# Attention feeding a squared-ReLU layer: batch 0's queries turned on TensorE and its second scores taken token-major

## The chip, the cores and the metric

The kernel runs on one core of a Trainium2 chip. A core has TensorE (PE in the profile; PEld is its weight load), VectorE (DVE), ScalarE (ACT), GpSimd (POOL) and SyncE (SP), each with its own in-order queue of instructions, a memory SBUF of 128 partitions, an accumulator memory PSUM that TensorE writes, and 16 DMA engines. The metric is the device time of one execution in microseconds (us), the median over several.

## The reference

```
def sm_attn(qq, kk, vv):                     # per batch (8) and head (8)
    s = scale * matmul(qq, kk.T)             # scale = 1/8
    a = softmax(s)                           # over the last axis
    return matmul(a, vv)
p_packed = sm_attn(p, k, v)                  # 32 packed queries against 576 tokens
attn     = sm_attn(q, p_packed, p_packed)    # 576 tokens against the 32 packed rows
x = attn.transpose(0, 2, 1, 3).reshape(4608, 512)
out = square(relu(x @ w_in)) @ w_out         # 512 -> 2048 -> 512
```

Each tensor q, k, v is 8 x 8 x 576 x 64 in float32, p is 8 x 8 x 32 x 64.

## The kernel before

**Tiling.** The eight heads of a batch are two quads of four. The 32 packed rows of four heads fill 128 partitions, so one quad is one tile. Tokens of a batch are 576 = 18 x 32 (S, T, NP). For batches 0 and 1 the tokens are cut into half A of 256 and half B of 320 (CUTS, line 40), for the others into two of 288.

**Stages of one batch.** k is turned on DVE in 32x32 blocks of 32-bit pairs (`kT`), first scores s1 on TensorE, their maximum `m1` on DVE, exponential `x1` on ACT with its sum, transpose `eT` on TensorE, copy `eo` out of PSUM, product with v `pv`, division `pp` (reciprocal `rd` before it). The packed rows pp are turned twice: `pt`/`po` give ppT through TensorE and a copy, `bd` gives ppd in 32x32 blocks on DVE. Then the second attention: q turned on DVE (`qA`, `qB` for the halves, line 363), second scores (`zA`, `zB`, line 375) with the packed rows on the partitions and the tokens along the free axis, a DVE transpose of the scores to have tokens on the partitions (`tA`, line 518), maximum `mA`, subtraction `sA`, exponential `xA`, sum and reciprocal `uA`, weighting `aA`, and a transpose back (`TA`, line 563) to a2T. These seven steps run once for each quad and half. The product of packed rows with w_in is formed once per batch (`wa`, `wb`, `w0`, `w1`, with copies `Wa` and so on), so that the first layer is `h` = wp x a2T: for each block of 128 features two matmuls, one a quad. `r` is the ReLU out of PSUM, `q` with dots the square into gT, `o` the second layer, two matmuls a word, `c` its copy and `d` the store.

**What sets the order.** ORDER (lines 50 to 132) is a list of words written out by hand, 1,451 of them; `run` executes them in this order, and each engine works its own instructions off in it. A letter behind the colon gives the engine (a ACT, p POOL, v or none DVE). A word such as `qA01` names the step, batch and quad; `h0.1.8` batch, half and feature block. `Z18.0` issues 18 matmuls on zeros of 512 columns and none of 256, which write to a PSUM bank that nobody reads (`busy`, line 333). Loads stand in the list too: `Lk`, `Lv`, `LA`/`LB` (q's halves), `Wi` (w_in in six pieces: column part 0, 1 or 2, then the row half), `Wo` (w_out in quarters) on POOL's queue, `pf` (p of the first two batches) on SP's. POOL's transfers use eight semaphores in turn, so a transfer is issued when the one eight places ahead of it has landed. The second layer of the first four token tiles takes w_out's quarters in the order 0, 2, 1, 3.

**PSUM.** Four banks of the pool `psa` make two double buffers (tag a) that s1, second scores and wp share; the other four hold small tiles and the zeros' target in the first stage (`spare`, `idle`), and later x and y for h and o. Batch 0's even blocks use x, its odd ones y.

Of the kernel before, what the change touches and what calls it, by code (L numbers as in the profile page):

```python
# [9 lines left out]
ALU = mybir.AluOpType  # L10
# [11 lines left out]
D = 64  # L22
# [12 lines left out]

WIDE = range(2, 8)
# [20 lines left out]
q0.1.0:v r0.1.8:a h0.1.10 W100:v W101:a h0.1.11 h0.1.3 q0.1.4:p h0.1.2 r0.1.10:a r0.1.3:v r0.1.11:a h0.0.4 kT10 r0.1.2:a  # L57
LB1 h0.0.13 r0.0.4:a h0.0.5 q0.1.1:a h0.1.14 r0.0.13:v q0.1.5:p h0.0.14 r0.0.5:v h0.1.13 r0.1.14:a kT11 h0.0.15
r0.0.14:a h0.0.6 q0.0.2:a h0.0.12 Wo1 r0.0.15:v s11 r0.1.13:a r0.0.12:v r0.0.6:a Wo3 h0.1.15 q0.0.7:v q0.0.6:a h0.0.7
r0.1.15:v h0.1.4 r0.0.7:a Lv20 h0.1.6 m110 r0.1.4:a h0.1.5 r0.1.6:a h0.1.7 m111 h0.1.12 q0.0.3:a o2.0 x110 r0.1.5:v o2.1  # L60
r0.1.12:v q0.1.7:p o0.0 x111 o3.0 r0.1.7:a eT10 q0.1.6:a o0.1 Pr q0.1.2:v eT11 q0.1.3:v eo10:a o1.0 rd1 eo11:v o3.1 pv1
o1.1 pp1 o0.2 pt1 o1.2 bd1 po1:a o3.2 qA11 w011 w111 qA10 W011:a o0.3 W111:v o2.2 Lv21 o1.3 qB10 zA1 qB11 w010 o2.3 tA11
W010:a tA10 o3.3 mA11 zB1 mA10 sA11 w110 o0.4 sA10 tB11 W110:a o2.4 tB10 o1.4 mB11 xA11 o0.5 xA10 mB10 o1.5 uA10 o2.5
Lk20 sB11 o0.6 uA11 o0.7 xB11 aA10 o1.6 c0:a aA11 o1.7 sB10 o3.4 TA10 c1:a d0 TA11 o2.6 uB11 xB10 h1.0.1 Lk21 h1.0.6 Px
o2.7 r1.0.1:v d1 r1.0.6:v o3.5 aB11 h1.0.0 c2:a h1.0.2 Pt o3.6 r1.0.0:a TB11 o3.7 r1.0.2:a d2 Lk31 Pu:v q1.0.0:a h1.0.4
h1.0.3 c3:a o4.0 r1.0.3:v r1.0.4:a o5.0 kT20 q1.0.1:a h1.0.7 d3 h1.0.5 uB10 o5.1 r1.0.5:a o4.1 r1.0.7:v q1.0.2:a aB10
h1.0.10 h1.0.8 q1.0.3:v r1.0.10:a o4.2 kT21 Lq2 h1.0.9 r1.0.8:a o5.2 r1.0.9:a h1.0.12 TB10 s12 q1.0.4:v r1.0.12:a
h1.0.14 m120 o5.3 Lv30 r1.0.14:a h1.1.1 m121 h1.1.3 r1.1.1:a o5.4 x120 r1.1.3:v h1.0.11 o4.3 r1.0.11:v x121 h1.1.7 kT31
h1.0.15 eT20 Lq3 q1.0.5:a o4.4 r1.0.15:v eT21 r1.1.7:v q1.0.7:a o5.5 rd2 eo20:v eo21:a h1.0.13 h1.1.2 r1.0.13:v o4.5
r1.1.2:v q1.0.6:a h1.1.6 pv2 r1.1.6:v h1.1.8 pp2 h1.1.0 q1.1.1:a r1.1.8:v Lk30 o5.6 qT21 q1.1.3:a o4.6 h1.1.12 r1.1.0:a  # L70
bd2 pt2 qT20 o4.7 bs2:a Lk40 h1.1.5 po2:v r1.1.12:a o5.7 q1.1.0:v c4:a h1.1.10 r1.1.5:v c5:a s22 d4 r1.1.10:v h1.1.4
o6.0 t221 r1.1.4:a h1.1.9 d5 o7.0 q1.1.2:a t220 h1.1.13 r1.1.9:a o6.1 qT30 r1.1.13:a Lq4 h1.1.11 q1.1.4:a m221 w120 w121
r1.1.11:a o6.2 m220 W121:a h1.1.14 h1.1.15 W120:v Lv31 o6.3 r1.1.14:a q1.1.6:a o7.1 o6.4 sb21:v r1.1.15:a Lv40 o7.2
q1.1.5:a kT30 o7.3 q1.1.7:a o7.4 sb20:v Lk41 x221 o6.5 qT31 o7.5 x220 o6.6 su21 o6.7 o7.6 su20 c6:a o7.7 w020 a221 c7:a
d6 w021 o8.0 W020:a a220 o8.1 d7 o8.2 aT21 W021:a o8.3 aT20 o8.4 Lq5 h2.0.1 h2.0.0 r2.0.1:v o8.5 r2.0.0:a o8.6 q2.0.0
h2.0.2 h2.0.3 r2.0.2:v o9.0 Lk50 o8.7 r2.0.3:v h2.0.5 c8:a s13 q2.0.1 r2.0.5:a h2.0.4 d8 m130 o10.0 r2.0.4:a h2.0.6 kT40
h2.0.7 r2.0.6:a o10.1 r2.0.7:a q2.0.2 h2.0.10 Lk51 x130 m131 o9.1 h2.0.8 r2.0.10:a q2.0.3 o9.2 r2.0.8:a kT41 h2.0.13
x131 eT30 h2.0.9 r2.0.13:v o10.2 eo30:a rd3 r2.0.9:v h2.1.1 eT31 q2.0.4 h2.0.14 r2.1.1:a o10.3 r2.0.14:v eo31:a h2.0.11
Lk61 o9.3 r2.0.11:v o9.4 h2.0.12 h2.1.5 q2.0.5 r2.0.12:a pv3 r2.1.5:v h2.0.15 q2.0.6 h2.1.4 pp3 r2.0.15:a o9.5 r2.1.4:v
h2.1.6 bd3 pt3 q2.0.7 h2.1.0 bs3:a o9.6 r2.1.6:v r2.1.0:v Lv41 po3:a o9.7 q2.1.2 h2.1.8 q2.1.0 c9:a h2.1.2 r2.1.8:v s23  # L80
# [54 lines left out]
class Kernel:  # L135
# [128 lines left out]
    def load_rows(self, x, s, n=0, engine=None):  # L264
# [558 lines left out]
```

## Time and profile before

| | |
|---|---|
| median of 3 runs | 243.33 us (243.23 to 243.66) |
| the profiled execution | 243.35 us, span from first to last instruction 241.5 us |
| busy time PE / DVE / ACT / POOL | 235.4 / 203.0 / 142.0 / 74.8 us |
| first 512-column matmul on zeros | 1.19 us |
| first product of the first layer (batch 0, half A) | 21.28 us |
| first product of half B | 24.45 us |
| first second-layer matmul (o2.0) | 33.0 us |
| first product of batch 1 (h1.0.1) | 48.8 us |
| matmuls on zeros (L335) | 59, 16.1 us |
| landing of k00, k01, v00, v01, q half A | 6.05, 7.7, 9.2, 10.65, 12.1 us |
| landing of w_in's four narrow pieces, q half B | 13.3, 14.6, 18.0, 19.3; 17.0 us |
| landing of w_out's quarters 0, 2, 1, 3 | 30.2, 35.6, 41.0, 43.5 us |

Starts are from the timeline, in us from the first instruction. A landing is the issue's start plus the time to landing in the view of transfers. Busy TensorE time includes the matmuls on zeros, so it does not tell how much of it is needed work. A wait on an engine that is not the bottleneck costs nothing.

### The profile page before, as it was taken

How to read it: one execution, taken by the hardware profiler on the slowest of the kernel's cores; microseconds unless marked ns; L12 is line 12 of the kernel's file. 1: busy time of each engine (PE TensorE's matmuls, PEld its weight loads, DVE VectorE, ACT ScalarE, POOL GpSimd, SP SyncE). 2: the span in 40 equal slices, each digit the busy share in tenths (PEclk: the TensorE clock that was granted, in tenths of full speed). 3: DMA queues.
4: the chain of work that ended last, by engine and by line, in shares of the span. 5: the costliest groups of instructions: out<-in, count | busy, mean ns of one | idle time of the engine just before them, and what ended most of it. 6: DMA issues, size and time to landing. Idle time of an engine off the chain costs nothing.

```text
span 241.5 us, 6098 instructions
## 1 busy us (share of the span) xinstructions
PE 235.4 (97%) x2415; PEld 125.9 (52%) x2415; DVE 203.0 (84%) x459; ACT 142.0 (59%) x308; POOL 74.8 (31%) x123
## 2 busy tenths in 40 slices
PE   8998899999999999999999999999999999999994
PEld 3544564456544564456555554465545644555542
DVE  2679986999998889989998889997899879987740
ACT  2216993697897557955693647774495346733300
POOL 8637783594585262044303340002000000000000
PEclk9999999999999999999999999999999999999999
DMA  6999999999999979259932974217113111111224
GB/s 103 189 199 210 202 206 206 181 209 210 194 169 212 236 103 136 51 71 209 107 86 28 206 107 66 62 34 105 37 24 76 46 46 43 43 46 43 50 61 109
DMA packets 33404, 28.51 MB, mean 118 GB/s; under 512 B 8160, under 2 KB 28384, under 8 KB 33376
## 3 DMA queue, kind: packets, MB, share of 16 engines
q0 software_dynamic: 26848, 18.55, 54.2%
q1 hardware_dynamic: 6384, 9.51, 14.8%
q8 instruction: 19, 0.31, 0.5%
q14 instruction: 9, 0.07, 0.1%
q10 hardware_dynamic: 144, 0.07, 0.1%
HBM read 37.22 MB, written 9.44 MB: 193 GB/s over the span
## 4 chain that ended last, share of the span: by engine, by line
PE 91%; DMA 4%; ACT 2%; DVE 1%; SPq 0%; issue 0%; POOL 0%; POOLq 0%
PE ps_o L648 50%; PE ps_h L590 26%; PE ps_wp L574 4%; PE ps_idle L335 3%; PE ps_s L375 3%; DMA k_b<-in_k_dram 2%; PE ps_e1T L433 2%; PE ps_pv L457 1%; DMA out_dram<-o_sb 1%; ACT r L595 1%; ACT wp L419 1%; SPq L679 0%; PE ps_ppT L496 0%; ACT gT L633 0%; DVE kT L351 0%
## 5 line engine op out<-in xcount | busy, mean ns | idle before, releaser
L648 PE MATMUL ps_o<-w_out_bf,gT 128*128 128x512 bf16 (+1 forms) x576 | 147.3, 378 | 0.0
L590 PE MATMUL ps_h<-a2T,wp 128*128 128x288 bf16 (+2 forms) x512 | 89.9, 286 | 1.3 <-DVE rs L543 0.6
L595 ACT ACTIVATE r<-ps_h 128x288 bf16<-128x288 f32 (+2 forms) x159 | 61.0, 415 | 47.2 <-PE ps_h L590 42.5
L648 PEld LDWEIGHTS <-gT 128*128 128x128 bf16 x576 | 54.4, 98 | 43.1 <-issue 3.4
L590 PEld LDWEIGHTS <-wp 128*128 128x128 bf16 x512 | 47.7, 98 | 42.4 <-issue 8.0
L597 DVE TENSOR_SCALAR r<-ps_h 128x288 bf16<-128x288 f32 (+2 forms) x97 | 41.9, 447 | 11.1 <-PE ps_h L590 10.5
L635 DVE TENSOR_TENSOR gT<-r 128x576 bf16<-128x576 bf16 (+2 forms) x104 | 45.1, 446 | 2.8 <-ACT r L595 1.8
L419 ACT CAST wp<-ps_wp 128x1024 bf16<-128x1024 f32 (+1 forms) x29 | 27.7, 974 | 9.0 <-PE ps_wp L574 8.9
L419 ACT COPY o_sb<-ps_o 128x512 f32<-128x512 f32 x26 | 15.2, 589 | 12.3 <-PE ps_o L648 10.1
L268 POOL DMA_DIRECT2D k_b<-in_k_dram x28 | 15.2, 544 | 16.5 <-DVE kT L351 7.3
L268 POOL DMA_DIRECT2D q_b<-in_q_dram x16 | 11.0, 690 | 28.8 <-DVE qT L363 25.4
L313 POOL DMA_DIRECT2D v_b<-in_v_dram x12 | 9.4, 779 | 31.5 <-PE ps_pv L457 30.5
L335 PE MATMUL ps_idle<-gT 128*128 128x512 bf16 (+1 forms) x59 | 16.1, 417 | 1.2 <-DVE gT L187 1.2
L413 ACT ACTIVATE e<-ps_s,nm 128x576 bf16<-128x576 f32 x16 | 11.8, 742 | 7.5 <-DVE nm L401 7.4
L633 ACT ACTIVATE gT<-r 128x512 bf16<-128x512 bf16 (+1 forms) x21 | 14.0, 690 | 0.5 <-DVE r L597 0.3
L535 ACT ACTIVATE e<-d 128x576 f32<-128x576 f32 (+2 forms) x20 | 11.7, 599 | 4.1 <-DVE d L529 3.9
L351 DVE STREAM_TRANSPOSE kT<-k_b 128x576 uint32<-128x576 uint32 x16 | 12.3, 767 | 0.6 <-DMA k_b<-in_k_dram 0.6
L363 DVE STREAM_TRANSPOSE qT<-q_b 128x576 uint32<-128x576 uint32 (+2 forms) x20 | 12.4, 633 | 0.0
L541 DVE TENSOR_REDUCE sums<-e 128x18 f32<-128x576 f32 (+2 forms) x20 | 12.2, 608 | 0.1
L401 DVE TENSOR_REDUCE nm<-ps_s 128x1 f32<-128x576 f32 x16 | 11.5, 739 | 0.8 <-PE ps_s L375 0.7
L523 DVE TENSOR_REDUCE mx<-s 128x18 f32<-128x576 f32 (+2 forms) x20 | 11.6, 609 | 0.0
L529 DVE TENSOR_TENSOR d<-s,mx 128x576 f32<-128x576 f32 (+2 forms) x19 | 11.6, 631 | 0.0
(60 smaller groups left out, 179.3 us busy)
## 6 DMA issues: line engine op xcount, KB each, us to landing
out_dram<-o_sb SPq DMA_DIRECT2D x65, 128.0 KB, 2.9
v_b<-in_v_dram POOLq DMA_DIRECT2D x12, 256.0 KB, 5.5
w_out_bf<-in_moe_w_out_dram POOLq DMA_DIRECT2D x4, 512.0 KB, 12.4
q_b<-in_q_dram POOLq DMA_DIRECT2D x6, 288.0 KB, 5.3
q_b<-in_q_dram POOLq DMA_DIRECT2D x12, 144.0 KB, 5.7
k_b<-in_k_dram POOLq DMA_DIRECT2D x12, 108.0 KB, 4.1
gT<-in_v_dram POOLq DMA_DIRECT2D x4, 288.0 KB, 9.7
w_in_bf<-in_moe_w_in_dram POOLq DMA_DIRECT2D x4, 256.0 KB, 9.8
```

The costliest lines, as they stand in the source:

```text
L268: engine.dma_start(x[n:], s[:P - n])
L335: self.nc.tensor.matmul(ps[:, :m], lhsT=self.nought[:, :P], rhs=self.nought[:, :m], start=True, stop=True)
L351: self.nc.vector.transpose(t["kT"][:].rearrange("p s e -> p (s e)").bitcast(U32), t["k"][:].rearrange("p t d -> p (t d)").bitcast(U32))
L363: self.nc.vector.transpose(out.bitcast(U32), x.bitcast(U32))
L419: engine.copy(out, x)
L541: nc.vector.reduce_sum(out=sums[:, x], in_=t["e2"][:, x], axis=AX.X)
L590: self.nc.tensor.matmul(ps, lhsT=t["wp"][:, fb // n, fb % n * P:(fb % n + 1) * P], rhs=t["a2T"][:, s0:s1], start=(qd == 0), stop=(qd == se ...
L595: engine.activation(r, ps, ACT.Relu)
L597: engine.tensor_scalar_max(r, ps, 0.0)
L633: engine.activation(out, r, ACT.Square)
L635: engine.tensor_tensor(out=out, in0=r, in1=r, op=ALU.mult)
L648: self.nc.tensor.matmul(self.o[tt][:, e], lhsT=self.gT[:, fb, a:a + P], rhs=self.w_out_bf[:, fb, e], start=(i == 0), stop=(i == self.NFB - 1))
```

## The change

Five things are changed.

1. **Queries of batch 0** are no longer turned on DVE. TensorE turns them with the identity into PSUM (`QA`, `QB`: 4 or 5 transposes for a quad and half) and a copy brings them to SBUF (`EA`, `EB`: three of the four on ACT, one on DVE). Two tokens of 64 features now fill the 128 partitions.
2. **Second scores of batch 0** (`yA`, `yB`) have 32 tokens of one head as weights and ppT as the moving operand, so that each matmul gives a block of 32 tokens x 32 packed rows with the tokens on the partitions. Half A takes 64 such matmuls and half B 80, in place of 16 each. The DVE transposes of the scores (`tA`, `tB`) and ppd of batch 0 (`bd`) are not made.
3. **The softmax** of batch 0's second attention runs for both quads in one instruction: `MA` maximum and `SA` subtraction straight from PSUM, `XA` exponential in place, `UA` sum and reciprocal, and the same for B. The exponentials are kept in float32 in an unused part of gT. Only the weighting `AA` is still one instruction a quad, all four now on DVE (three of the four were on POOL, with one subtraction).
4. **The early part of ORDER** is new, up to the first words of batch 1's first layer: 269 words become 259, and the last 1,182 words are the same steps on the same engines. p's first loads are split: batch 0's on ACT's queue ahead of its table load, batch 1's on SP's. On POOL's queue the order is k00, k01, q half A, v00, v01, q half B, the six pieces of w_in, then batch 1's k, w_out's first quarter, and batch 1's v and q. There are 24 matmuls on zeros in place of 59.
5. **Other engines** for some batch 0 steps: an e1T copy and a wp copy go to ACT and ppT's copy to DVE, and several ReLUs and squares change places between ACT, DVE and POOL.

The functions that are new:

```diff
+    def st_qP(self, t, qd, hf):
+        n = self.span(hf)
+        x = self.q_part(t["q"], n)[:, qd]
+        m = (n.stop - n.start) // 2
+        ps = t["ps_q", hf] = self.bank16(0, "ps_q")[:, :m * P].rearrange("p (u c) -> p u c", c=P)
+        for u in range(m):
+            self.nc.tensor.transpose(ps[:, u, :], x[:, 2 * u:2 * u + 2, :].rearrange("p t d -> p (t d)"), self.ident)
+
+    def st_qE(self, t, engine, hf):
+        n = self.span(hf)
+        y = self.new(t, self.tp, "qT", [P, T // 2, P], BF16)
+        self.copy(engine, y[:, n.start // 2:n.stop // 2, :], t["ps_q", hf])
+
+    def st_z(self, hf):
+        n = self.span(hf)
+        m = (n.stop - n.start) // 2
+        ps = self.turn32("ps_z")[:, :, :self.NQ * m * NP].rearrange("p e (q u i) -> p e q u i", q=self.NQ, i=NP)
+        self.att[0, 0]["ps_z", hf] = ps
+        for u in range(m):
+            for qd in range(self.NQ):
+                t = self.att[0, qd]
+                for h in range(QH):
+                    g = NP * self.group(qd, h)
+                    for e in range(2):
+                        r = slice(D * e, D * e + D)
+                        self.nc.tensor.matmul(ps[g:g + NP, e, qd, u, :],
+                                              lhsT=t["qT"][r, n.start // 2 + u, NP * h:NP * h + NP],
+                                              rhs=t["ppT"][r, NP * h:NP * h + NP], start=True, stop=True)
+
+    def st_zmax(self, hf):
+        ps = self.att[0, 0]["ps_z", hf]
+        self.nc.vector.tensor_reduce(out=self.z_small("mxz", hf), in_=ps, op=ALU.max, axis=AX.X)
+
+    def st_zsub(self, hf):
+        ps, d = self.att[0, 0]["ps_z", hf], self.z_work(hf)
+        self.nc.vector.tensor_tensor(out=d, in0=ps, in1=self.z_small("mxz", hf).unsqueeze(4).to_broadcast(list(d.shape)), op=ALU.subtract)
+
+    def st_zexp(self, hf):
+        d = self.z_work(hf)
+        self.nc.scalar.activation(d, d, ACT.Exp, scale=SCALE)
+
+    def st_zsum(self, hf):
+        x, y = self.z_small("smz", hf), self.z_small("rsz", hf)
+        self.nc.vector.reduce_sum(out=x, in_=self.z_work(hf), axis=AX.X)
+        self.nc.vector.reciprocal(y, x)
+
+    def st_za2(self, engine, hf, qd):
+        t, n = self.att[0, qd], self.span(hf)
+        e2, rs = self.z_work(hf)[:, :, qd], self.z_small("rsz", hf)[:, :, qd]
+        a2 = self.new(t, self.tp, "a2", [P, T // 2, NP, 2], BF16)
+        engine.tensor_tensor(out=a2[:, n.start // 2:n.stop // 2].rearrange("p u i e -> p e u i"), in0=e2,
+                             in1=rs.unsqueeze(3).to_broadcast(list(e2.shape)), op=ALU.mult)
```

`z_work` is the float32 view of gT, `z_small` a small tile for each half. The order, up to half B's first product and the words just behind it:

```diff
-pf Lk00 Lk01 Lv00 Lv01 I P0 LA0 P1 Wi00 kT00 Wi10 LB0 Z18.0 s100 Wi01 kT01 Wi11 m100 Z2.0 s101 x100 m101 Wi21 x101 Z7.0
-eT00 eo00:v Z1.0 eT01 rd0 eo01:v Wi20 Z2.0 pv0 pp0 qA01 Lk10 Z2.0 pt0 bd0 qA00 po0:a Z2.1 zA0 Lk11 tA00 tA01 mA01 mA00
-sA01:v xA01 sA00:v uA01 xA00 qB00 Wo0 qB01 aA01:p uA00 Z18.1 zB0 wa00 Lv11 tB00 tB01 aA00:p Wa00:a mB00 Z2.1 wa01 mB01
-sB00:p Wa01:a TA01 Z1.1 wb01 TA00 Lv10 wb00 xB00 sB01:v h0.0.8 h0.0.9 Wb01:a Wb00:v h0.0.1 h0.0.0 xB01 uB00 r0.0.8:a
-r0.0.1:a h0.0.2 uB01 r0.0.9:a aB00:p r0.0.0:a h0.0.3 r0.0.2:v q0.0.4:a h0.0.11 Wo2 aB01:v h0.0.10 q0.0.0:a TB00 TB01
-r0.0.3:a r0.0.10:v r0.0.11:a h0.1.0 h0.1.1 q0.0.1:v q0.0.5:a h0.1.9 r0.1.0:v h0.1.8 r0.1.1:a r0.1.9:v LA1 w100 w101
...
+pf1 pf0 Lk00 P0 Lk01 P1 LA0 Lv00 I kT00 kT01 Z14.0 s100 s101 m100 m101 x100 QA00 Z1.1 eT00 Lv01 x101 rd0 Z0.1 eT01
+eo01:v eo00:a Z2.0 pv0 pp0 LB0 EA00:a QA01 EA01:a pt0 po0:v Z0.1 yA0 Z0.1 QB00 MA0 QB01 EB01:v EB00:a Wi00 SA0 Wi01 Z1.0
+yB0 Wi10 Wi11 Wi20 XA0 MB0 wa01 UA0 Wa01:a Z1.1 wa00 SB0 AA00:v AA01:v wb01 Wa00:a TA00 TA01 wb00 XB0 Wb01:a h0.0.1
+h0.0.0 Wb00:a h0.0.2 UB0 r0.0.0:a Wi21 r0.0.1:a h0.0.3 r0.0.2:a h0.0.11 AB00:v AB01:v h0.0.8 Lk11 h0.0.10 Lk10 TB00 TB01
+Wo0 r0.0.3:a q0.0.1:v r0.0.11:a r0.0.8:a h0.0.9 r0.0.9:a h0.1.11 h0.1.0 r0.0.10:v h0.1.9 q0.0.0:v h0.1.10 r0.1.11:a Lv11
+Lv10 Wo2 h0.1.1 r0.1.0:v r0.1.9:a r0.1.1:a h0.1.8 q0.0.4:v r0.1.10:v h0.1.3 w100 q0.0.5:v w101 r0.1.3:a W100:v r0.1.8:a
...
```

More of the change, by code (lines that the diff above doesn't have):

```diff
@@ L270, in load_rows, with k_first, k_cast @@
             engine.dma_start(x[:n], s[P - n:])
+    def k_first(self, hf):
+        y = WIDE_CUTS[hf]
+        s = self.k[0, :QH].rearrange("h (l t) d -> (h l) t d", t=T)
+        self.nc.sync.dma_start(self.k_f[:, y, :], s[:, y, :])
+    def k_cast(self, engine, hf):
+        y = WIDE_CUTS[hf]
+        t = self.att.setdefault((0, 0), {})
+        self.copy(engine, self.new(t, self.ld, "k", [P, T, D], BF16, "k_b")[:, y, :], self.k_f[:, y, :])
     def load_q(self, b, hf=None):
@@ new lines, in z_work, with z_small @@
+    def z_work(self, hf):
+        m = (self.span(hf).stop - self.span(hf).start) // 2
+        r = 2 + 4 * hf
+        return self.gT[:, r:r + 4, 3 * S:3 * S + 2 * m * NP].bitcast(F32).rearrange("p (e q) (u i) -> p e q u i", e=2, i=NP)
+    def z_small(self, name, hf):
+        m = (self.span(hf).stop - self.span(hf).start) // 2
+        return self.new(self.att[0, 0], self.sm, (name, hf), [P, 2, self.NQ, T // 2], F32, name)[:, :, :, :m]
+    def st_zmax(self, hf):
+        ps = self.att[0, 0]["ps_z", hf]
+        self.nc.vector.tensor_reduce(out=self.z_small("mxz", hf), in_=ps, op=ALU.max, axis=AX.X)
@@ L612, in step_r, with step_f @@
         self.relu(engine, self.r[b, hf, fb // 2][:, fb % 2, :s1 - s0], self.ph.pop((b, hf, fb))[:, :s1 - s0])
+    def step_f(self, engine, b, hf, fb):
+        s0, s1 = self.part(b, hf)
+        ps, c = self.ph.pop((b, hf, fb))[:, :s1 - s0], (b % 4) * S
+        self.nc.vector.scalar_tensor_tensor(out=self.gT[:, fb, c + s0:c + s1], in0=ps, scalar=0.0, in1=ps, op0=ALU.max, op1=ALU.mult)
     def step_hh(self, engine, b, hf, fp):
```

212 lines of the change are left out of this document (122 added, 90 removed).

## The prediction

> **What bounds the kernel now.** First the page's head and its chain of waits; then the busy time by stretch; then the timeline of the first 25 us; then the groups by shape and the transfers.
>
> ```profile
> span 241.5 us, 6098 instructions
> ...
> PE 91%; DMA 4%; ACT 2%; DVE 1%; SPq 0%; issue 0%; POOL 0%; POOLq 0%
> ```
>
> The chain that ends last is TensorE almost throughout: a microsecond is saved only where TensorE is not yet doing needed work. The stretches say where that is (columns: PE, PEld, DVE, ACT, POOL busy, granted clock, DMA share, GB/s):
>
> ```profile
> 0.00:10.00 10.00, 8.75 (x72) 3.75 (x73) 4.39 (x12) 2.07 (x3) 8.04 (x17) 1.00 0.86 135
> 10.00:21.30 11.30, 11.18 (x164) 5.13 (x162) 8.67 (x27) 3.21 (x9) 5.85 (x11) 1.00 1.33 202
> 21.30:30.00 8.70, 7.42 (x70) 4.55 (x64) 8.54 (x21) 8.59 (x23) 6.09 (x8) 1.00 1.21 207
> 30.00:45.00 15.00, 15.00 (x232) 7.50 (x231) 11.88 (x29) 10.10 (x22) 8.06 (x11) 1.00 1.36 201
> ```
>
> From 30 us on TensorE has no idle time. Between 21.3 and 30 it has 1.28 us, and DVE (8.54 of 8.70) and ACT (8.59) are full. Before 21.3 its busy time is largely filler:
>
> ```profile
> 8.59 0.69 PE L375 MATMUL ps_s<-kT,pT 32*32 32x192 bf16 x24
> ...
> 12.15 0.64 PE L457 MATMUL ps_pv<-gT,e1T 96*32 96x64 bf16 x48
> ...
> 14.15 0.42 PE L375 MATMUL ps_s<-qT,ppd 32*32 32x256 bf16 x16
> 14.50 4.17 PE L335 MATMUL ps_idle<-gT 128*128 128x512 bf16 x19
> 18.60 0.48 PE L375 MATMUL ps_s<-qT,ppd 32*32 32x320 bf16 x16
> ...
> 21.28 1.03 PE L590 MATMUL ps_h<-a2T,wp 128*128 128x256 bf16 x8
> ...
> 24.45 1.56 PE L590 MATMUL ps_h<-a2T,wp 128*128 128x320 bf16 x8 [0.35 <-DVE a2T L563]
> ```
>
> So batch 0's attention is a latency chain: second scores of half A at 14.15, first layer product at 21.28; scores of half B at 18.60, its first product at 24.45. From first score to first product, half A takes 7.1 us and half B 5.9 us, most of it DVE's.
>
> **The change, part by part.** Prices of single instructions come from the groups by shape:
>
> ```profile
> L401 DVE TENSOR_REDUCE nm<-ps_s 128x1 f32<-128x576 f32 x16 | 11.5, 739 | 0.8 <-PE ps_s L375 0.7
> ...
> L529 DVE TENSOR_TENSOR d<-s,mx 128x576 f32<-128x576 f32 x12 | 8.7, 745 | 0.0
> ...
> L541 DVE TENSOR_REDUCE sums<-e 128x18 f32<-128x576 f32 x12 | 8.8, 730 | 0.0
> ...
> L421 DVE COPY e1T<-ps_e1T 128x640 bf16<-128x640 bf16 x6 | 2.9, 480 | 0.3 <-PE ps_e1T L433 0.3
> ...
> L535 ACT ACTIVATE e<-d 128x576 f32<-128x576 f32 x12 | 8.3, 703 | 0.2 <-DVE d L529 0.2
> ```
>
> By the same groups' 256 and 320 forms, 64 more elements cost DVE about 0.07 us. A group of two is 0.05 to 0.09 shorter than twice one, so a follower with its inputs there starts about 0.08 before its predecessor ends; across engines I add 0.06, and 0.14 more behind a matmul group (pv's 0.64 ends at 12.79, pp starts at 12.87).
>
> *Taken from DVE* (batch 0): four q transposes (1.77), ppd (0.22), four score transposes (1.78), four maxima (1.7), three subtractions (1.3), four sums with reciprocals (2.5), one a (0.5), one e1T copy (0.55) and one wp copy (0.68): 11.0. *Given to it*: MA 0.68 and MB 0.81 (512 and 640 elements, from the 576 row), SA 0.68, SB 0.81, UA and UB with reciprocals 0.92 and 1.08, four a2 (2×0.42, 2×0.51), one qT copy 0.48, ppT 0.28: 7.6. DVE: -3.4. ACT loses four exp (1.8) and ppT (0.37) and gains XA 0.65, XB 0.76, three qT copies (0.58, 0.58, 0.69), an e1T copy 0.80 and a wp copy 0.58: +2.5. POOL loses its four softmax instructions (2.7). TensorE gains 18 transposes (55 ns each: the e1T groups run 6 in 0.33) and 144 score matmuls in place of 32, and loses 35 of its 59 filler matmuls.
>
> *The price without a row* is that of the 144 matmuls (64x32 weights, 32 columns). Lower bound: pv, 48 matmuls of 64 columns in 0.53 to the next group, 11 ns each. Upper: the first scores, 24 in 0.62, 26 ns. They work as pv does, with neighbours in other column groups, so I take 12.5 ns: yA0 0.80, yB0 1.00.
>
> [...]
>
> *Transfers.* POOL's queue is dense, so a slot's landing depends on what lies ahead:
>
> ```profile
> q_b<-in_q_dram POOLq DMA_DIRECT2D x1, 256.0 KB, 7.7
> ...
> q_b<-in_q_dram POOLq DMA_DIRECT2D x1, 320.0 KB, 10.5
> ```
>
> Issued at 4.38 and 6.48, these land at 12.1 and 17.0; k01 lands at 7.7, v00 at 9.2, v01 at 10.65, the four narrow w_in pieces at 13.3 to 19.3. The new order is k00, k01, qA, v00, v01, qB, w_in: qA lands about 9.1, v00 10.6, v01 12.1 (the same bytes are ahead as were through qA), qB about 13.8, and the last narrow w_in again 19.3, since the set before it is the same. On ACT the first p transfer (64 KB) is issued ahead of the table load, both done long before the first exp at 9.21. SP keeps its three small transfers, so P1, at 5.99 before, should stay.
>
> *Walk to half A's product.* Up to x101 (10.12 to 10.86) nothing on the path changes. eT01 then no longer stands behind filler (11.29 before): 10.97; eo01, no longer behind eo00 on DVE, 11.50; pv's second part waits for v01, 12.16; pp0 12.62 (12.87 before), ppT ready 13.71, yA0 13.77 (14.15 before): -0.38. Then 0.80+0.20 to MA 14.77; EB01 on DVE, which stands ahead of SA and waits for QB01, 15.48; SA 15.88; XA 16.62; yB0 starts when EB01 is done, 16.02, and MB at 17.22; UA 17.95, its reciprocal 18.67; SB 18.85; two AA from 19.58, two TA from 20.26; product at 20.80: -0.5 against 21.28. qB could land 0.9 late before QB00 (14.67) is held.
>
> *Half B.* XB 19.72 on ACT; UB 20.66, reciprocal 21.52, AB from 21.86, TB from 22.72; product at 23.32, against 24.45: -1.1. That the long filler and the wait for qB (17.0) are gone is the larger part.
>
> *Onward.* To the first product of batch 1 both orders hold the same work, on other engines. I walked both in-order queues with these prices, PSUM buffers and landings included: 47.1 after, 48.2 before (the trace has 48.8; the 0.6 the walk lacks I take as common). Shift: -1.1. Margins on the way are thin: Wi11 0.4 us before wb01, k10 0.4 before kT10, w_out's first quarter (30.2) 0.6 before o2.0, and q of batch 1 (36.9) is already what qA11 waits for; with that wait DVE holds ppd and the second scores of batch 1, which TensorE reaches only at 38.4. From there the same words follow, with no DVE wait on a transfer after 47.5 us in this trace, so the shift stays. Sum: 243.35 (profiled execution: span 241.5 and 1.85 around it; median 243.33) - 1.1 = 242.25. With all new DVE and ACT instructions 0.1 us longer or shorter the walk moves +0.7 or -0.4; with matmuls at 11 ns by -0.2.
>
> **Rivals.**
>
> *Small matmuls at the first scores' price.* 144 × 13.5 ns = 1.9 us, all on the chain, since SA and MB wait for the groups: walk -1.1+1.8 = 0.7 slower, 244.05. It decides from 20 ns per matmul up (there the gain is nil). For it: the 24-matmul row. Against: pv, twice (12.15 and 36.82). [...]
>
> *The clock falls.* The first filler matmuls, until 5.4 us, start 0.43 us apart; later 512-column ones run 0.22 apart: half speed for the first 4.2 us of work. The new order leaves TensorE about 50 to 70% busy from 6 to 20 us, with gaps up to 1.4 us; before, its sparsest 3.4 us had 63% by my walk and nothing slowed. If half speed returned: eT01 +0.3, pv +0.3, the scores +1.8, and up to +1.7 on products: 2 to 4 us, 244.3 to 246.3. For it: no such thin stretch has been run at full speed in this trace. Against: no gap near the 4 us of warming. [...]
>
> *Late transfers.* v01, k01 and the loads with thin margins count one for one beyond them; 0.6 to 1.2 us late eats the gain: 242.85 to 243.75. For: DMA busy share over 1.2 throughout. Against: the sets ahead of the critical slots are as before.
>
> **How the numbers follow.** Forecast as summed (241.75 to 242.75): 0.58. More gain than that: 0.04. Late transfers: 0.13. Small matmuls dear: 0.12. Clock: 0.12. The remaining 0.01 lies in slower. What this kernel's measurement can tell from no change is about 0.2%, 0.49 us. Faster 0.62, same 0.13, slower 0.25. The range 241.6 to 244.3 takes in the forecast, late transfers and dear matmuls, and leaves out most of the clock case.
>
> **What would show it.** yA0 near 0.8 us; first products near 20.8 and 23.3; batch 1's first product near 47.7 by the trace; no q transposes on DVE in front; v01 landing at about 12.1. Wrong if: 64-matmul groups take over 1.3 us, the first wide products run 0.2 us a 256-column matmul, or products stall on w_in or w_out.

## The result and the profile after

| | before | after |
|---|---|---|
| median | 243.5 us (243.23 to 243.71, 4 runs) | 245.91 us (245.49 to 246.51, 4 runs) |
| ratio to before | | 1.0101, 95% interval 1.0073 to 1.013 |
| the profiled execution | 243.35 us, span 241.5 us | 245.55 us, span 243.8 us |
| first score matmul of half A | 14.15 us | 13.46 us |
| first score matmul of half B | 18.60 us | 15.38 us |
| first product of the first layer | 21.28 us | 21.79 us |
| first product of batch 1 | 48.80 us | 50.80 us |

The changed kernel is slower by 1.0%, where 0.45% faster was forecast. These are the lines of its page that answer to the head and the chain of waits of before, with the row of the granted TensorE clock (one digit for each 6.1 us, in tenths of full speed):

```profile
span 243.8 us, 6235 instructions
...
PEclk9995999999999999999999999999999999999999
...
PE 86%; DVE 6%; issue 3%; DMA 2%; ACT 1%; POOL 0%; ACTq 0%; DVEq 0%; POOLq 0%
```

The clock row of the kernel before:

```profile
PEclk9999999999999999999999999999999999999999
```

Two things are new: a 5 in the clock row, and "issue" with 3% of the chain, which is time in which an engine waited for nothing that the profile shows. The busy time by stretch (PE, PEld, DVE, ACT, POOL busy; granted clock, DMA share, GB/s), cut as it was for before, has the clock in its two middle rows:

```profile
0.00:10.00 10.00, 7.23 (x75) 3.53 (x75) 4.88 (x12) 2.59 (x4) 8.14 (x17) 1.00 0.89 138
10.00:21.30 11.30, 7.09 (x255) 4.22 (x254) 6.01 (x13) 5.02 (x10) 4.40 (x7) 0.87 1.34 202
21.30:30.00 8.70, 7.47 (x64) 4.50 (x58) 7.83 (x19) 7.25 (x18) 3.22 (x4) 0.78 1.20 205
30.00:45.00 15.00, 13.74 (x212) 7.20 (x214) 10.26 (x26) 10.45 (x24) 8.64 (x13) 1.00 1.34 201
```

TensorE now has 1.26 us of idle time even between 30 and 45 us, where it had none. TensorE's timeline tells where the chain broke (start, length, instruction, count; in brackets the idle time ahead of it and what ended it):

```profile
13.46 0.65 PE L405 MATMUL ps_z<-ppT,qT 64*32 64x32 bf16 x64 [0.27 <-DVE ppT L510]
...
15.38 0.27 PE L405 MATMUL ps_z<-ppT,qT 64*32 64x32 bf16 x9 [0.29 <-ACT qT L508]
17.66 0.71 PE L405 MATMUL ps_z<-ppT,qT 64*32 64x32 bf16 x71 [2.01 <-issue]
18.20 0.45 PE L663 MATMUL ps_wp<-w_in_bf,ppT 64*32 64x256 bf16 x8
...
21.79 5.55 PE L679 MATMUL ps_h<-a2T,wp 128*128 128x256 bf16 x30 [0.47 <-DVE a2T L652]
27.27 0.63 PE L663 MATMUL ps_wp<-w_in_bf,ppT 64*32 64x512 bf16 x16
...
29.03 1.56 PE L679 MATMUL ps_h<-a2T,wp 128*128 128x256 bf16 x12 [0.76 <-DVE wp L510]
31.69 0.71 PE L679 MATMUL ps_h<-a2T,wp 128*128 128x256 bf16 x4 [1.10 <-ACT r L684]
```

Up to 15.38 the chain runs ahead of the forecast. Then TensorE does nine of the 80 score matmuls of half B, stands for 2.01 us though both operands are ready, and does the other 71 in one go. After that the first 30 products take 5.5 us to the next group, 0.18 us each; the first eight of the kernel before took 1.03 us, 0.13 each. In all thirteen traces the rows of the granted clock last 3.41 us or a multiple of it (13.65 and 6.83 us here), but for the last, which the end cuts off; so in these traces the granted clock changes only at moments a multiple of 3.41 us apart. The stretches between those moments show why it fell (same columns as above):

```profile
14.84:18.25 3.41, 1.11 (x88) 0.75 (x87) 1.14 (x3) 1.12 (x2) 1.19 (x2) 1.00 1.43 198
18.25:21.67 3.42, 2.33 (x50) 0.73 (x39) 3.17 (x8) 1.96 (x4) 1.50 (x3) 0.50 1.26 210
21.67:25.08 3.41, 3.29 (x16) 1.97 (x16) 2.92 (x9) 2.89 (x8) 0.78 (x2) 0.50 1.17 207
```

The stretch with the stall has TensorE busy for 1.11 us. The two after it run at half speed.

**The stall.** Counted from the start of TensorE's program (a matmul is two instructions, its weight load and itself: x75 of each from 0 to 10 us above), the stall lies ahead of instruction 447 or 448. The trace has 19 transfers of kind "instruction" on one queue, 16 KB each:

```profile
q8 instruction: 19, 0.31, 0.5%
```

TensorE's 5,020 instructions over 19 are 264 a transfer, so about 256 a block, which is also the distance between the two places where kernels stall here and below, 447 and 703. That the queue is TensorE's is borne out by the runs below: the kernel before, with 4,830 instructions, has 19 transfers there too, and the two kernels with 5,080 and 5,078 (e1 and e2) have 20. The trace's records give when each began. Late in the kernel, where the DMA engines have time (DMA share 0.13 from 141.87 to 142.52 us, 0.17 from 165.18 to 165.96), block n begins within about a microsecond of the moment when TensorE passes instruction 256n-79 (from -0.1 to +1.1 us for blocks 12 to 19 of the changed kernel). Read with that rule, the first blocks stand so:

| kernel, block | asked for (passed 256n-79) | transfer | TensorE reaches 256n+191 |
|---|---|---|---|
| before, 1 | 11.57 | 14.95 to 15.90 | 20.70, no wait |
| before, 2 | 20.26 | 23.74 to 24.68 | 31.54, no wait |
| after, 1 | 11.61 | 15.29 to 16.23 | 15.65, goes on at 17.66 |
| after, 2 | 15.39 | 21.29 to 22.23 | 26.09, no wait |

The theory (code supply): a block is asked for about 270 instructions ahead of its first instruction, waits 3.4 to 5.9 us in the full DMA engines (DMA share 1.25 to 1.38 in the four waits of the table), takes 0.95 us, and can be used 1.4 us later, in all some 6 us. The kernel before takes 9.1 us for those 270 instructions. The changed one takes 4.0, because 73 of the tiny matmuls, 146 instructions that run in 0.7 us, lie in there, and the long run of fillers is gone. The rivals: the matmuls waited for operands or banks of their own; and, for the clock, that it is lost for want of fillers, whatever the stall.

### The profile page after: what moved, and what is told of

Same layout as the page of the kernel before. It is cut to its first block, busy times and chain, and to the rows that moved or that the text cites. A ratio compares the mean times of both kernels' runs of the same rounds, so it can differ in the third digit from the quotient of the medians.

```text
span 243.8 us, 6235 instructions
## 1 busy us (share of the span) xinstructions
PE 228.6 (94%) x2476; PEld 125.2 (51%) x2510; DVE 200.4 (82%) x445; ACT 145.6 (60%) x312; POOL 70.9 (29%) x118
## 4 chain that ended last, share of the span: by engine, by line
PE 86%; DVE 6%; issue 3%; DMA 2%; ACT 1%; POOL 0%; ACTq 0%; DVEq 0%; POOLq 0%
PE ps_o L743 49%; PE ps_h L679 27%; PE ps_wp L663 3%; PE ps_s L464 3%; DMA k_b<-in_k_dram 2%; PE ps_e1T L522 2%; PE ps_pv L546 2%; DVE kT L374 1%; PE ps_z L405 1%; DVE gT L730 1%; DVE mx L612 1%; PE ps_ppT L585 1%; DVE d L618 0%; PE ps_o L748 0%; ACT e L502 0%
## 5 line engine op out<-in xcount | busy, mean ns | idle before, releaser
L743 PE MATMUL ps_o<-w_out_bf,gT 128*128 128x512 bf16 (+1 forms) x543 | 141.4, 378 | 1.9 <-issue 0.3
L684 ACT ACTIVATE r<-ps_h 128x288 bf16<-128x288 f32 (+2 forms) x163 | 62.5, 413 | 49.9 <-PE ps_h L679 43.3
L686 DVE TENSOR_SCALAR r<-ps_h 128x288 bf16<-128x288 f32 (+2 forms) x93 | 40.4, 450 | 12.4 <-PE ps_h L679 11.6
L276 POOL DMA_DIRECT2D k_b<-in_k_dram x28 | 15.2, 544 | 16.7 <-DVE kT L374 9.8
L728 ACT ACTIVATE gT<-r 128x640 bf16<-128x640 bf16 (+1 forms) x19 | 12.8, 696 | 0.5 <-DVE r L686 0.5
L663 PE MATMUL ps_wp<-w_in_bf,ppT 64*32 64x512 bf16 (+1 forms) x272 | 11.1, 382 | 0.7 <-ACT wp L508 0.7
L624 ACT ACTIVATE e<-d 128x576 f32<-128x576 f32 (+2 forms) x16 | 10.1, 639 | 2.1 <-DVE d L618 2.1
L278 POOL DMA_DIRECT2D k_b<-in_k_dram x19 | 9.9, 520 | 4.4 <-DMA q_b<-in_q_dram 2.4
L638 DVE TENSOR_TENSOR a<-e,rs 128x576 bf16<-128x576 f32 (+2 forms) x16 | 10.9, 703 | 0.0
L452 DVE STREAM_TRANSPOSE qT<-q_b 128x576 uint32<-128x576 uint32 (+2 forms) x16 | 10.8, 682 | 0.0
L630 DVE TENSOR_REDUCE sums<-e 128x18 f32<-128x576 f32 (+2 forms) x16 | 10.5, 657 | 0.0
```

The lines of the kernel that those rows point to most:

```text
L663: self.nc.tensor.matmul(ps[NP * g:NP * g + NP, c, :f1 - f0], lhsT=t["ppT"][D * c:D * c + D, NP * h:NP * h + NP], rhs=self.w_in_bf[D * c:D ...
L684: engine.activation(r, ps, ACT.Relu)
L686: engine.tensor_scalar_max(r, ps, 0.0)
L728: engine.activation(out, r, ACT.Square)
L743: self.nc.tensor.matmul(self.o[tt][:, e], lhsT=self.gT[:, fb, a:a + P], rhs=self.w_out_bf[:, fb, e], start=(i == 0), stop=(i == self.NFB - 1))
```

## The experiments

**e1_shift: the same fillers, more instructions.** A new word `Y` issues matmuls on zeros of 128 columns.

```
- ... kT01 Z14.0 s100 ...
+ ... kT01 Z4.0 Y40 s100 ...
```

> The changed kernel with its first 14 fillers of 512 columns written as 4 of 512 and 40 of 128: the same columns, 60 more instructions ahead of everything else on TensorE. Theory (code supply): TensorE's program comes in 16 KB blocks of 256 instructions; the block that begins at its instruction 447 is asked for at about instruction 177 (11.61 us) and can be used at 17.66, 6.05 us later, and the changed kernel gets to 447, the tenth matmul of the second half of the scores, at 15.65. With 60 more ahead the 2.01 us stall inside the second half of the scores is gone; the limit now falls near the end of the first half (asked for at about 8.4, usable at 14.5, at most 0.6 us of wait there) and again at the last w_in products (asked for at about 13.9, usable at 20 or later, about 1 us). The window from 14.8 to 18.2 us is then busier than 2 us and the clock stays 1.00: 242.6 to 244.2 us. Rival (the matmuls wait for their own operands or banks): 2.0 us of stall stays inside the second half of the scores, 245.9 us. Rival (clock lost for want of fillers, whatever the stall): the stall is gone and the clock is 0.50 for 6.8 us all the same, about 244.5 to 245.5 us.

Measured: 245.27 us, ratio 1.0086 (1.0065 to 1.0106), span 243.3 us. TensorE's timeline:

```profile
16.55 0.80 PE L418 MATMUL ps_z<-ppT,qT 64*32 64x32 bf16 x80 [0.29 <-ACT qT L521]
...
20.01 0.41 PE L676 MATMUL ps_wp<-w_in_bf,ppT 64*32 64x256 bf16 x8 [0.37 <-DMA w_in_bf<-in_moe_w_in_dram]
20.98 0.41 PE L676 MATMUL ps_wp<-w_in_bf,ppT 64*32 64x256 bf16 x7 [0.56 <-issue]
```

All 80 matmuls of half B now run in one group, so it was not theirs. A wait for nothing appears where the theory put the next boundary: ahead of instruction 703, after the first matmul of the last w_in group (block 2: asked for at 14.86, moved 18.70 to 19.60, used at 20.98). The time came out a microsecond above the theory's range, and the clock fell all the same, for one stretch (20.80 to 24.21), after one in which TensorE was busy for 1.66 us. The rival for the clock had that time right. The fillers of 128 columns also took longer, so that the first scores started 0.69 us later (7.55 us against 6.86).

**e2_before_tiny: the stall put into the kernel before.** `V130` issues 130 matmuls of 32 columns on zeros.

```
- ... aA01:p uA00 Z18.1 zB0 ...
+ ... aA01:p uA00 V130 Z12.1 zB0 ...
```

> The kernel before with 6 of its 18 fillers ahead of the second half of the scores written as 130 fillers of 32 columns, which take about the same 1.3 us: 248 more instructions there, nothing else changed. Code supply: the block from instruction 703 is then asked for at about 16.6 us and needed at the last w_in products near 20.8; it is usable 6 to 8 us after it is asked for, so TensorE waits 1.2 to 3.6 us there for nothing that the profile shows, and the time is 244.3 to 246.5 us. Rival (instructions cost nothing but their own time): no such wait, 243.2 to 243.9 us.

Measured: 246.25 us, ratio 1.013 (1.0092 to 1.0168). TensorE's timeline:

```profile
14.60 0.64 PE L348 MATMUL ps_idle<-gT 64*32 64x32 bf16 x62
17.50 0.69 PE L348 MATMUL ps_idle<-gT 64*32 64x32 bf16 x68 [2.26 <-issue]
...
19.09 3.75 PE L335 MATMUL ps_idle<-gT 128*128 128x512 bf16 x11 [0.22 <-issue]
```

The kernel before, with 124 more matmuls that read only zeros and wait for nobody, stalls for 2.26 us after 62 of its tiny ones: the 62nd is its instruction 446. The rival falls. The time lies in the theory's range, but the place was wrong: the wait was expected at 703, at the last w_in products, and came at 447. The theory itself has it there: block 1 is asked for at 11.67 us, and the tiny matmuls bring TensorE to 447 by 15.06. In the profiled execution part of the loss is my own fillers: the clock fell (busy 1.05 us in the stretch) and eleven of them took 0.34 us each in place of 0.22, ahead of the scores of half B. The four executions part the two causes: two kept a granted clock of 1.000 and took 245.40 and 245.51 us, two fell to 0.993 and took 246.98 and 247.27. So here the stall with its extra instructions costs about 2.2 us over the kernel before (243.30) with the clock kept, and one half-speed stretch 1.7 us more. Only one of the four has a trace; that the others stalled alike is inferred from their times.

**e3_half: half as many score matmuls.** Both token parities in one matmul of 128 rows and 64 columns, on a block-diagonal copy of ppT (`pD0`, `pD1`, two copies more).

```
-  for e in range(2):
-      r = slice(D * e, D * e + D)
-      matmul(ps[g:g+NP, e, qd, u, :], lhsT=qT[r, u, head], rhs=ppT[r, head])
+  matmul(ps[g:g+NP, qd, :, u, :], lhsT=qT[:, u, head], rhs=ppD[:, qd, :, head])
```

> The changed kernel with the two token parities of the second scores in one matmul: 72 matmuls of 128 rows by 64 columns in place of 144 of 64 by 32, on a block-diagonal copy of the turned pv product (two more copies of 64 by 256 elements); 144 fewer instructions. Code supply: instruction 447 is then the first w_in product after the scores, near 16.0 us; the block is usable at about 17.7, so the wait moves behind the scores, 1.0 to 1.7 us, where it delays only the w_in products; the second scores end by 16.5 instead of 18.2, the first product starts at 20.0 to 20.8, 242.0 to 243.6 us; the window around the wait is busier than 2 us and keeps the clock. Rival (operands or banks of the scores): a stall of about 2 us stays inside the second half of the scores, 245.5 us or more.

Measured: 245.77 us, ratio 1.0109 (1.0084 to 1.0133). TensorE's timeline:

```profile
15.73 0.54 PE L405 MATMUL ps_z<-gT,qT 128*32 128x64 bf16 x40 [0.29 <-ACT qT L513]
16.41 0.27 PE L668 MATMUL ps_wp<-w_in_bf,ppT 64*32 64x256 bf16 x1
17.91 0.30 PE L668 MATMUL ps_wp<-w_in_bf,ppT 64*32 64x256 bf16 x7 [1.23 <-issue]
...
20.59 6.08 PE L684 MATMUL ps_h<-a2T,wp 128*128 128x256 bf16 x30
```

The stall moved to the first w_in products, again at instruction 447, and the first product came at 20.59, 0.7 us earlier than before. That and the places were as the theory had it. The time was not: the stretch with the stall was busy for 1.75 us, the clock fell for two stretches, and the 30 products took 6.0 us. A lead of 0.7 us at the first product ended as a loss of 1.9 us at batch 1's first product (50.72 us).

**e5_before_sparse: the clock alone.** The kernel before without its longest run of fillers; few instructions, no stall.

```
- ... aA01:p uA00 Z18.1 zB0 ...
+ ... aA01:p uA00 zB0 ...
```

> The kernel before without the 18 and a half fillers ahead of the second half of the scores: TensorE has nothing to do for about 4 us from 16 to 20 us. Clock theory: the 3.41 us window in there is busy less than 1.2 us, the granted clock is 0.50 for one or two windows after it, the first products take 0.217 us in place of 0.108, and the time is 244.8 to 246.5 us. If the clock doesn't follow the fillers: 243.2 to 243.9 us.

Measured: 243.84 us, ratio 1.0036 (1.0015 to 1.0058). Stretches (columns as above):

```profile
16.15:19.56 3.41, 1.20 (x26) 0.47 (x26) 3.17 (x10) 0.86 (x3) 2.11 (x4) 1.00 1.36 201
19.56:22.98 3.42, 3.42 (x35) 1.23 (x34) 2.98 (x9) 2.62 (x6) 1.97 (x3) 0.50 1.25 208
```

The clock fell as expected, without any stall, but the time is only 0.9 us longer by the ratio (span 241.9 us, 0.4 longer), where at least 1.5 was expected. The clock was back at 22.98; the half-speed stretch held fillers, w_in products and only the first microsecond of products. The ten executions lie in two groups by their granted clock: six with 0.990 to 0.992, as in this profile (one half-speed stretch), took 243.22 to 243.86 us, and four with 0.985 or 0.986 (two stretches' worth) 244.35 to 245.36. Over the kernel before (243.30) that is about 0.5 us for one stretch and 1.8 for two; the forecast (244.8 to 246.5) fits three of the second group's four.

**e6_half_shift and e7_warm: stall away, then clock kept.** Both on the kernel of e3.

```
- ... kT01 Z14.0 s100 ...                    e6 and e7
+ ... kT01 Z7.0 Y28 s100 ...
- ... wa01 UA0 Wa01:a Z1.1 wa00 SB0 AA00:v AA01:v wb01 Wa00:a TA00 TA01 wb00 ...      e7 alone
+ ... wa01 UA0 Wa01:a Z4.0 wa00 SB0 AA00:v AA01:v Z3.0 wb01 Wa00:a TA00 TA01 Z2.0 wb00 ...
```

> The kernel with 72 score matmuls, and 42 instructions more ahead of everything (7 of its 14 first fillers of 512 columns written as 28 of 128). Code supply: the block from instruction 447 is asked for at about 9.4 us instead of 11.7 and is usable at about 15.4; instruction 447 is now in the second half of the scores at about 15.9, so no wait for nothing of more than 0.4 us is left before 30 us. Clock: from the windows seen so far, one that is busy 1.79 us or more of 3.41 keeps the clock and one of 1.75 us or less loses it; with the stall gone the window from about 14.8 is above that, the next one (18.2 to 21.6) is near the limit. 243.0 to 245.0 us, against 245.77 with the stall. If the stall were harmless: 245.5 to 246 us.

> The same with 7 and a half more fillers of 512 columns between the w_in products (1.6 us of work into TensorE's idle time from 16.5 to 20 us): every window from 8 to 25 us is busy over 1.8 us and the granted clock stays 1.00 to the end. If the half-speed stretch costs what its matmuls lose beside the evictions (the squares and relus of ScalarE and VectorE limit part of it), 0.7 to 1.5 us come back: 242.3 to 243.8 us. If the clock is not what costs: within 0.3 us of the kernel without these fillers.

Measured: 245.13 us, ratio 1.0068 (1.0045 to 1.009), and 244.05 us, ratio 1.0028 (1.0018 to 1.0039). In e7 instruction 447 is reached at 15.93 us, after its block can be used. In e6 it is reached at 16.20, just before: TensorE stands for 0.21 us ahead of it. Neither list of TensorE's waits has an "issue" left before 30 us, and e6's time lies 0.1 us above the theory's range. In e6 the clock still fell, after a stretch busy for 1.92 us, which refutes the limit of 1.79 that I had read from the runs before. With 7.5 fillers more it stayed at 1.00, and the time fell by 1.1 us, as much as the theory had (0.7 to 1.5), though e7 itself lies 0.25 us above its range: so half speed cost about 1.1 us here. TensorE's timeline of e7:

```profile
20.13 0.61 PE L615 MATMUL ps_h<-a2T,wp 128*128 128x256 bf16 x4
20.91 3.67 PE L615 MATMUL ps_h<-a2T,wp 128*128 128x256 bf16 x26 [0.17 <-ACT wp L444]
...
25.21 0.62 PE L599 MATMUL ps_wp<-w_in_bf,ppT 64*32 64x512 bf16 x15 [0.32 <-DMA w_in_bf<-in_moe_w_in_dram]
...
26.96 1.56 PE L615 MATMUL ps_h<-a2T,wp 128*128 128x256 bf16 x12 [0.75 <-ACT wp L444]
29.62 0.71 PE L615 MATMUL ps_h<-a2T,wp 128*128 128x256 bf16 x4 [1.10 <-ACT r L620]
```

No stall, full clock, the first product 1.15 us earlier than before, and the kernel is still not faster. The lead goes between 21 and 30 us: TensorE waits for the wide w_in block, for its copy out of PSUM, and for a relu. From the first product to batch 1's first product it is idle for 2.73 us (29.19 less 26.46 busy), in the kernel before for 1.28 (27.52 less 26.24). The products themselves are hardly slower than there (26 in 3.6 us, 0.14 each, where the first eight of the kernel before took 0.13).

**e8_warm_squares and e9_squares: the wait for the relu.** e8 on e7's kernel, e9 on the changed one.

```
- ... h0.0.12 kT10 r0.0.15:a h0.1.13 r0.1.14:a q0.1.1:v s11 h0.0.7 q0.1.0:v r0.0.12:a ...
+ ... h0.0.12 r0.0.15:a h0.1.13 r0.1.14:a q0.1.1:v q0.1.0:v kT10 s11 h0.0.7 r0.0.12:a ...
```

> The same with two squares of batch 0 (q0.1.1, q0.1.0) put ahead of the second turn of batch 1's keys on VectorE, as ScalarE's relu waits 1.36 us for the buffers that they free and TensorE 1.10 us for that relu at 31 us. If that wait is on the path: 0.5 to 1.1 us less than the kernel without it. If something later ends last anyway: no change over 0.3 us.

> The changed kernel with nothing but these two squares ahead of that turn. If the wait of 1.10 us at 31.7 us is on the path: 244.8 to 245.5 us, against 245.91. If it is not, or comes back as a wait for the turned keys: 245.6 to 246.2 us.

Measured: 243.70 us, ratio 1.0015 (1.0003 to 1.0027), whose interval overlaps e7's; and 246.88 us, ratio 1.0137 (1.012 to 1.0154). Neither is what was expected. The wait stayed, at 1.01 and 0.97 us, as the squares, at their new place, run beside two of POOL's and take 1.46 and 1.42 us for the two in place of 0.85 (below). Of the 0.39 us by which e8 leads e7 behind that wait (29.23 against 29.62), 0.30 was there before it, at the wide w_in block, which landed at 24.87 in place of 25.17. e9's stall was also longer, 2.50 us, so its loss says little of the squares.

**e10_tail: the old late part behind the repaired early part.** From the first product to batch 1's first product, the words of the kernel before, on its engines; up to batch 1's v the loads keep the repaired kernel's order but for batch 1's k; those behind are in the order of before.

```
- ... XB0 Wb01:a h0.0.1 h0.0.0 Wb00:a h0.0.2 UB0 r0.0.0:a Wi21 ... AB00:v AB01:v ... TB00 TB01 Wo0 ...
+ ... XB0 Wi21 Lk10 Lk11 Wo0 Lv11 Lv10 h0.0.8 h0.0.9 Wb01:a Wb00:a h0.0.1 h0.0.0 UB0 ... AB00:p ... AB01:v ... TB00 TB01 r0.0.3:a ...
```

> The repaired kernel (72 score matmuls, 42 early instructions, 7 and a half fillers between the w_in products: no stall, clock 1.00, first product 20.3 us), with the words from its first layer-1 product to batch 1's first product in the order and on the engines of the kernel before. In the repaired kernel itself the first product came 0.97 us earlier than before and the end 0.23 us later: 1.2 us are lost between 20 and 33 us. Theory (the new order of the late part costs them: VectorE and ScalarE are busy there without a gap, and POOL has lost four multiplications and a subtraction to VectorE): with the old late part 242.2 to 243.1 us. Rival (the last narrow w_in block and batch 1's keys land at 24 to 28 us in either and end last, so an earlier first product is worth nothing): 243.3 to 244.0 us.

Measured: 243.11 us, ratio 0.9978 (0.9964 to 0.9993), span 241.5 us. TensorE's timeline:

```profile
20.45 2.27 PE L615 MATMUL ps_h<-a2T,wp 128*128 128x256 bf16 x16
23.63 1.34 PE L615 MATMUL ps_h<-a2T,wp 128*128 128x320 bf16 x8 [0.91 <-DVE a2T L588]
...
25.70 0.62 PE L599 MATMUL ps_wp<-w_in_bf,ppT 64*32 64x512 bf16 x15 [0.41 <-DMA w_in_bf<-in_moe_w_in_dram]
```

The same group in the kernel before, which waits for nothing there:

```profile
25.93 0.62 PE L574 MATMUL ps_wp<-w_in_bf,ppT 64*32 64x512 bf16 x16
```

Both readings hold a part. The old late part is worth about 0.6 us against e8 by the medians. But of the lead of 0.83 us at the first product, still 0.82 at half B's (23.63 against 24.45), only 0.23 is left at the wide w_in products (the group starts in earnest at 25.70, at 25.93 in the kernel before), where TensorE waits for the transfer, and just that is left of it at the later matmuls (0.24 to 0.26 us earlier). The spans of the two profiled executions are equal.

**e11_pool: two instructions given back to POOL.** On the kernel of e8.

```
- AB01:v ... q0.1.7:a
+ AB01:p ... q0.1.7:p
```

> The repaired kernel with its own late part, and two things given back to POOL: one of the two multiplications of the second half (AB01) and one square (q0.1.7). If the load on VectorE and ScalarE is what loses the 1.2 us: 0.3 to 0.8 us less than the repaired kernel (243.70), 242.9 to 243.4 us. If not the load but the order, or the transfers: 243.5 to 244.0 us.

Measured: 245.27 us, ratio 1.0072 (1.0046 to 1.0098). A miss that decides little: TensorE waited longer for a relu (1.25 us) and for batch 1's keys (0.96), the stretch from 27.78 was busy for 1.37 us, and the clock fell at 31.19. The price of the load alone can't be read from it; but its two fastest executions, at a granted clock of 0.996 and 1.000, took 244.36 and 244.47 us, so with the clock all but kept the gain that the theory had did not show either.

**e12_later: is the lead worth anything?** e10 with `Z4.0` in place of `Z2.0` ahead of `wb00`.

> The kernel with the repaired early part and the old late part, with two more fillers (0.43 us) ahead of the last w_in product before the first layer-1 product, so that the first product starts at about 20.9 us instead of 20.45, still 0.4 us ahead of the kernel before. Theory (the wide w_in block lands at about 25.6 us whatever the kernel does, TensorE waited 0.41 us for it, and the lead ends there): the first product is 0.4 us later, the wait for that transfer goes, and the end and the time stay within 0.15 us of 243.11. Rival (the lead of the first product is carried to the end one for one): 243.4 to 243.6 us and a span 0.4 us longer.

Measured: 243.04 us, ratio 0.9995 (0.998 to 1.0011), span 241.2 us. TensorE's timeline:

```profile
20.76 2.27 PE L615 MATMUL ps_h<-a2T,wp 128*128 128x256 bf16 x16
...
25.21 0.81 PE L599 MATMUL ps_wp<-w_in_bf,ppT 64*32 64x512 bf16 x16
```

The first product is 0.31 us later and the span 0.3 us shorter: the wide w_in block landed at 25.36 us in this execution, in e10's at 25.65, and the matmuls behind it run earlier by that difference (26.25 there, 25.96 here). The rival falls: a later first product does not come out at the end. It is not so that the block lands at the same time whatever the kernel does: it landed at 24.34 in the kernel before, at 24.76 in the changed one, and at 24.87 to 25.65 in e7, e8, e10 and e12; why it came later there is open. e10 and e12 are the best versions found; against the kernel before their intervals reach from 0.36% faster to 0.11% slower.

## Why the prediction was wrong

- **The price without a row** (12.5 ns a small matmul, bounds 11 and 26): right in kind, even too high. 64 start within 0.58 us (13.46 to 14.04), 9 ns each. The rival of dear matmuls falls.
- **Transfers** up to 20 us: right. q half A, v00, v01 and q half B landed at 8.96, 10.37, 11.84 and 13.73 us (forecast 9.1, 10.6, 12.1, 13.8), the last narrow w_in piece at 19.46 (19.3). The one wait of TensorE for them was 0.32 us, for q half A.
- **Walk to half A's product**: right in its order up to yB0, and 0.3 to 0.6 us early (yA0 13.46 for 13.77, yB0 15.38 for 16.02). **The step that failed first is the next one, "yB0 starts when EB01 is done, 16.02, and MB at 17.22"**: it priced 80 matmuls by their own time. They also need their code: the block with instruction 447 landed at 16.23, and TensorE went on only at 17.66. This took 2.01 us, moved MB to 18.47 and the first product to 21.79 (forecast 20.80). Half A was held up with half B: UA, which its product needs, had its input at 16.67, but stands behind MB in VectorE's queue and started at 19.21. e1, e2 and e3 show the cause: the same wait at instruction 447, or 256 later, with other work there, in two kernels.
- **The clock** was a rival with a chance of 0.12, set aside because no gap came near 4 us. That reason was wrong: the walk had TensorE 50 to 70% busy, the stall and smaller gaps left it busy for 1.11 of 3.41 us, 33%, and that was enough. The stretches that lost the clock in the thirteen traces were not idle: TensorE was busy in them for 0.80 (e9) to 1.92 us (e6). Its size was somewhat overrated: 2 to 4 us were written down. Executions of one kernel that differ in the clock give 1.7 us for one half-speed stretch (e2), and about 0.5 for one and 1.8 for two (e5, against the kernel before); e6 against e7 gives 1.1. The changed kernel lost two stretches (granted clock 0.985 or 0.986) in all four executions, so its own price was not measured.
- **"Onward ... Shift: -1.1"**: the second step that failed, and the one that would have spoilt the forecast without stall and clock. A lead at the first product was carried to batch 1 one for one. In e7 it is 1.15 us at the first product and batch 1 starts 0.5 us later than before; in e10 0.83 becomes 0.25; in e12 0.52 stays 0.53, and its first product is later than e10's. So it is not the first product that sets batch 1's start. By TensorE's waits in e7 and e10, what sets it between 21 and 30 us is what VectorE and ScalarE take out of PSUM, and the wide w_in block, which lands near 25.2 to 25.7 us in the runs that waited for it. No run moved that block alone, so the share of each is argued from the waits. The margins that the prediction listed (Wi11, k10, w_out) did not have this one; the rival of late transfers had the kind, with other blocks.
- **The sum**: +2.3 us of span in place of -1.1. Taken off one after the other, the medians fall by 0.8 us with the stall (after to e6, which also has half the score matmuls; the intervals of the two overlap), 1.1 with the clock (e6 to e7), and about 0.9 with the new late part (e7 to e10, the squares of e8 within it), together 2.8, against a loss of 2.4: e10 stands 0.3 us below the kernel before by the medians. Each step's worth holds in this order alone: in e2, with the old late part and the clock kept, the stall with its extra instructions costs about 2.2 us.

## What to carry to other kernels

Count a stage's instructions beside its time: a burst of tiny matmuls was cheap by its rows here (9 ns each) and still outran the supply of code while transfers filled the DMA engines (2.01 us of wait, in a stretch with a DMA share of 1.43), and a wait released by "issue" at a fixed count of instructions (447 in four kernels, 703 in e1) was the sign of it. Fillers that look like waste may be what keeps the clock (7.5 more of them did in e7, worth 1.1 us); before cutting them, work out TensorE's busy share over each 3.41 us, the step of the clock's rows here. When executions of one kernel scatter, sort them by their granted clock first: in e2 and e5 that gave the clock's price without a new kernel. And before a shorter chain is credited to the end, ask what else lands or is full where the chain ends.

## What the runs showed of the hardware

- **Code supply.** About 6 us from asking to use while the DMA share is 1.38 to 1.43 (e1, e3 and the changed kernel: transfer 3.7 to 3.8 us after asking, 0.9 us long, used 1.4 to 1.5 us after its end). That the wait in front of the transfer comes from the full DMA engines is argued from the later blocks of the changed kernel: 9 and 10 still wait 3.4 us, at a DMA share of 1.26 and 1.01, and 12 to 19 start within 1.1 us. No run emptied the engines early.
- **The clock's limit** lies near half of a stretch in these traces. Over all thirteen kernels, one profiled execution each, in the stretches of the first 40 us, every one with TensorE busy for at most 1.37 us of 3.41 lost full speed and every one with at least 2.03 kept it; between them four kept it (1.57 to 1.88) and three lost it (1.66, 1.75, 1.92), so busy time by the profile does not decide it alone. Half speed ended after a stretch busy for 3.19 us or more and went on after 2.33 to 2.71.
- **VectorE beside POOL.** In e8 the first of two squares on VectorE starts at 27.65 while POOL is at a square of its own until 28.35; it ends at 28.70, 0.35 us after POOL's, having taken 1.05. The second, with POOL done, takes 0.48. In e9 the first also ends 0.35 us after POOL's (31.90 and 31.55) and the two take 1.42 us; in the changed kernel, with POOL done, they take 0.85. So the order tried in e8 and e9 paid next to nothing: 0.09 us of the relu's wait in e8 (1.01 against 1.10). What holds VectorE's square up beside POOL's was not shown. e8's rows of VectorE and POOL:

```profile
27.65 1.05 DVE L666 TENSOR_TENSOR gT<-r 128x640 bf16<-128x640 bf16 x1
```

```profile
25.88 2.47 POOL L666 TENSOR_TENSOR gT<-r 128x640 bf16<-128x640 bf16 x2
```
